# A two-layer gated convolution and MLP on one core: compact table, DMA-turned k, and a 64-row inverse

## The chip, the cores and the metric

The kernel runs on one core of one Trainium2 chip. The metric is the device time of one execution in microseconds (us), as the median over several runs. The core has a matrix engine (PE; its weight loads are listed apart as PEld), a vector engine (DVE), a scalar engine (ACT), GpSimd (POOL) and a sync engine (SP), which here issues nearly all DMAs in one queue. Each engine takes its instructions in the order in which they were written; engines wait for one another through semaphores.

## The reference, cut to what matters

Sequence length is 2048, width 512, MLP width 1376; all arrays are bf16.

```python
def A(q, k, v, shift_k, ssm_k, ssm_D):             # gated long convolution
    kv = causal_conv4(k, shift_k) * v              # 4 taps along the sequence
    y  = irfft(rfft(pad(kv)) * rfft(pad(ssm_k).T)) # causal convolution of length 2048, per channel
    return q * (y + kv * ssm_D)

def B(x, w1, b1, w2, b2):                          # MLP
    return gelu(layernorm(x) @ w1 + b1) @ w2 + b2

x = A_q
for layer in range(2):
    x = x + A(layernorm(x), A_k, A_v, A_shift_k, A_ssm_k, A_ssm_D)
    x = x + B(layernorm(x), B_w1, B_b1, B_w2, B_b2)
```

The long convolution doesn't depend on x, so that both layers use the same y. It is computed once.

## The kernel before, in words

**Halves.** The sequence is split into two halves of 1024 positions. The convolution is done by Fourier transforms of both halves, written as small matrix products; the first half of y needs only the first half of k and v, the second needs both. Positions are held as 128 partitions by 8 slices of 512 channels.

**Stages of the convolution.** For each half, tags name the stages:

- `ht0`, `ht1`: the filter `ssm_k` is turned by PE transposes (`turn`, line 536) and evicted from PSUM.
- `h1`, `x1` (`stage1`, line 553): first transform stage of the filter (h) and of the data (x): 8 tiles of 16 matmuls of 128 columns each, one eviction of 128x1024 for each tile.
- `h2`, `x2` (`stage2`, line 565): second transform stage, 8 tiles of 16 matmuls with 64 moving columns. Its weights are 128 blocks of 128x128 out of the second-stage table at `R_S2` (16,384 columns, 4 MB), which is mostly zeros: it holds, for each of 8 channels of a group, the same small rotation, in the rows and columns of that channel alone. Tile t reads 2,048 columns of it.
- `swap` (line 586 on): eight 256 KB DMAs that exchange the partitions of the real and the imaginary part of the filter's transform.
- products: DVE multiplies the two transforms (line 464, 128x1024).
- `i1` (`inverse1`, line 665): 8 tiles of 16 matmuls, 128 rows by 128 columns, with the small matrix `R_U` as moving operand; `i2` (`inverse2`, line 683): 16 matmuls of 512 columns. y of the half is then in `R_YT`.

**The short convolution.** For the first half, k is loaded by four DMAs in its natural layout and turned by 32 PE transposes (`shift_turn`, line 585) with four evictions; `shift` (line 610) does the four taps as 22 matmuls for each of four channel blocks, and DVE multiplies the result by v (line 616). For the second half, k arrives already turned, by eight transposing DMAs (line 766), and `shift_pair` (line 638) works on 32-row tiles.

**The layers.** When y of a half is there, the two layers run in blocks of 1, 2 or 4 slices (`BLOCKS`): statistics on DVE (lines 797, 798) with a power on POOL (line 804), normalization on ACT or DVE (lines 822, 823), gate and sum on DVE (line 464, 128x512), a second normalization, turning by PE or DMA, then `m1` (line 886, 44 matmuls) with the activation on ACT (line 891), and `m2` (line 920, 11 matmuls of 512 columns for each slice) with the sum on DVE (line 924). Half 0 runs its blocks while the convolution of half 1 is computed between them.

**What sets the order.** Every operation is recorded with its reads and writes by a small planner, `Prog`. The order of all operations (`SEQ`), the engine of those that may go to more than one (`ENGS`: a for ACT, v for DVE, p for POOL) and the PSUM bank of each tile (`BANKS`) are literal lists in the file; `arrange` places the operations in that order on their engines, `sync` derives the semaphore waits. So a new order is a new set of the three lists.

Of the kernel before, what the change touches and what calls it, by code (L numbers as in the profile page):

```python
# [7 lines left out]
ALU = mybir.AluOpType  # L8
# [28 lines left out]
class Prog:  # L37
# [60 lines left out]
    ENGS = ("apvpvvvpavaavaaaaaavvvaaavvvpvpvaavaaaaavaavvaaaaaaaavavaaaaaavaaavaaaaaappppaaaaaaaaaaaaaaaaaaaaaaaaaaaaapvvp"  # L98
            "paappvppaappvvvpaappaappaappaappaappaappvavpaappvappaappvvppvvvpaappvvavvvvvvavpvvvvppavavpvvvvvpvaaavpvvaaapv"
            "avva")  # L100
    BANKS = ("02220326464004602026041320002442462264542202240064064646402046462667062260046446220462640604660406064226644472"
             "44450442172316353547502206314500451400554567076567013226140174645320543403764701436154766316307007062272260403"
# [243 lines left out]
def _tables():  # L346
# [5 lines left out]
    a = np.arange(8)  # L352
# [608 lines left out]
```

## Time and profile before

| what | value |
|---|---|
| median of 3 runs | 239.39 us (238.99 to 239.71) |
| profiled execution: span from first to last instruction | 238.6 us |
| PE / DVE / ACT / POOL busy share of the span | 95% / 75% / 67% / 23% |
| DMA moved | 26.75 MB, 15.07 MB read from HBM |
| the 16 loads of the second-stage table | 256 KB each, 9.0 us from issue to landing |

The page gives the span of the profiled execution, not its device time; the median of the runs is 0.8 us longer than that span. A busy share counts an engine as busy while any of its instructions is under way; matmuls are pipelined, so that an instruction's recorded duration is much longer than the distance to the next, and distances are read from the chain or from the timeline (time of a run of instructions divided by their count). The first `m1` matmul starts 60.40 us after the span's start. In the stretch before, PE is busy in part; after it, up to 236.2 us, PE works nearly without a gap.

### The profile page before, as it was taken

To read this page: it belongs to the slowest core of one execution; us is meant where nothing else is said; L and a number is where in the kernel's file an instruction comes from. 1 tells how busy PE (TensorE), PEld (TensorE's weight loads), DVE (VectorE), ACT (ScalarE), POOL (GpSimd) and SP (SyncE) were. 2 spreads that over 40 slices of the span, in tenths; PEclk is the share of its full clock that TensorE was granted. 3 is DMA by queue.
4 is the path that set the end of the run, shared out by engine and by line. 5 is a ranking of instruction groups with operands and counts; after the bars stand their busy time and mean duration, and the time that the engine had idled before them with its cause. 6 is when DMAs were issued, how large, how long until landed. Compare 5 with 4: busy or idle time off the path is not lost.

```text
span 238.6 us, 6251 instructions
## 1 busy us (share of the span) xinstructions
PE 226.9 (95%) x2615; PEld 152.3 (64%) x2637; DVE 178.1 (75%) x358; ACT 159.6 (67%) x255; POOL 55.3 (23%) x120
## 2 busy tenths in 40 slices
PE   6998698899999999999999999999999999999995
PEld 3897588885968588667769675644445444444454
DVE  0579869999999999999999999593579469404013
ACT  2586879999996899999768786359036606831630
POOL 2421030104623506446004522303020210200000
PEclk9999979999999999999999999999999999999999
DMA  6999767989946660053100304200300050132202
GB/s 173 350 393 388 272 181 186 257 267 194 163 87 197 153 140 3 1 69 103 54 0 15 80 0 83 49 3 12 78 0 3 18 157 0 25 66 91 84 0 91
DMA packets 41112, 26.75 MB, mean 112 GB/s; under 512 B 23702, under 2 KB 33788, under 8 KB 41084
## 3 DMA queue, kind: packets, MB, share of 16 engines
q1 hardware_dynamic: 40786, 26.20, 40.5%
q8 instruction: 21, 0.34, 0.6%
q10 hardware_dynamic: 298, 0.16, 0.3%
q14 instruction: 7, 0.06, 0.1%
HBM read 15.07 MB, written 2.10 MB: 72 GB/s over the span
## 4 chain that ended last, share of the span: by engine, by line
PE 83%; DVE 6%; DMA 4%; ACT 3%; issue 2%; POOL 1%; SPq 1%; POOLq 0%
PE ps L886 32%; PE ps L920 31%; PE ps L665 6%; PE ps L553 5%; PE ps L565 3%; ACT ar L469 3%; DMA ar<-in_A_ssm_k_dram 2%; DVE ar L464 2%; DMA ar<-ar 2%; DVE ar L616 1%; PE ps L683 1%; PE ps L909 1%; PE ps L638 1%; PE ps L610 1%; DVE ar L470 1%
## 5 line engine op out<-in xcount | busy, mean ns | idle before, releaser
L891 ACT ACTIVATE ar<-ps,sm 128x256 bf16<-128x256 f32 (+4 forms) x143 | 65.4, 525 | 41.0 <-PE ps L886 39.5
L469 ACT ACTIVATE ar<-ps 128x1024 bf16<-128x1024 f32 (+3 forms) x77 | 71.3, 1005 | 16.4 <-PE ps L553 6.4
L886 PE MATMUL ps<-ar 128*128 128x256 bf16 (+4 forms) x568 | 81.5, 297 | 0.3
L920 PE MATMUL ps<-ar 128*128 128x512 bf16 (+1 forms) x324 | 77.2, 379 | 1.1 <-issue 0.3
L886 PEld LDWEIGHTS ps<-ar 128*128 128x128 bf16 (+1 forms) x572 | 52.8, 100 | 28.1 <-ACT ar L891 0.4
L464 DVE TENSOR_TENSOR ar<-ar 128x512 bf16<-128x512 bf16 (+3 forms) x105 | 62.7, 637 | 0.9 <-ACT ar L469 0.4
L920 PEld LDWEIGHTS ps<-ar 128*128 128x128 bf16 (+1 forms) x341 | 32.4, 98 | 33.4 <-ACT ar L891 0.2
L924 DVE TENSOR_TENSOR ar<-ar,ps 128x512 bf16<-128x512 bf16 x31 | 20.7, 678 | 33.2 <-PE ps L920 33.0
L797 DVE BATCH_NORM_STATS2 sm<-ar 128x6 f32<-128x512 bf16 x64 | 42.9, 683 | 0.5
L822 ACT ACTIVATE ar<-ar,sm 128x512 bf16<-128x512 bf16 x34 | 26.4, 811 | 9.5 <-DVE sm L809 8.3
L804 POOL TENSOR_TENSOR sm<-sm 128x2 f32<-128x2 f32 (+2 forms) x26 | 23.6, 909 | 23.8 <-DVE sm L802 22.0
L802 POOL TENSOR_SCALAR sm<-sm 128x2 f32<-128x2 f32 (+2 forms) x21 | 6.4, 304 | 97.3 <-DVE sm L798 97.1
L553 PE MATMUL ps<-ar 128*64 128x128 bf16 x512 | 18.6, 227 | 3.1 <-issue 1.4
L565 PEld LDWEIGHTS ps<-ar 128*128 128x128 bf16 x512 | 18.4, 102 | 3.4 <-ACT ar L469 1.0
L565 PE MATMUL ps<-ar 128*128 128x64 bf16 x512 | 19.6, 199 | 0.5 <-ACT ar L469 0.4
L553 PEld LDWEIGHTS ps<-ar 128*64 128x64 bf16 x512 | 15.7, 114 | 6.1 <-issue 2.6
L812 POOL TENSOR_SCALAR sm<-sm 128x1 f32<-128x1 f32 x43 | 16.1, 390 | 2.0
L470 DVE CAST ar<-ps 128x1024 bf16<-128x1024 f32 x11 | 13.3, 1222 | 4.3 <-PE ps L565 2.8
L665 PE MATMUL ps<-ar 128*128 128x128 bf16 x256 | 15.0, 219 | 0.5 <-DVE ar L464 0.4
L665 PEld LDWEIGHTS ps<-ar 128*128 128x128 bf16 x256 | 14.7, 113 | 1.2 <-DVE ar L464 0.6
L823 DVE TENSOR_SCALAR ar<-ar,sm 128x512 bf16<-128x512 bf16 x30 | 11.8, 410 | 3.4 <-POOL sm L812 3.1
L470 DVE COPY ar<-ps 128x1024 bf16<-128x1024 bf16 (+1 forms) x9 | 5.5, 632 | 8.0 <-PE ps L516 5.3
(41 smaller groups left out, 94.3 us busy)
## 6 DMA issues: line engine op xcount, KB each, us to landing
ar<-tab_s SPq DMA_DIRECT2D x16, 256.0 KB, 9.0
ar<-ar SPq DMA_DIRECT2D x16, 256.0 KB, 3.7
ar<-in_A_ssm_k_dram SPq DMA_DIRECT2D x8, 256.0 KB, 6.8
ar<-in_A_q_dram SPq DMA_DIRECT2D x8, 256.0 KB, 4.7
ar<-in_A_v_dram SPq DMA_DIRECT2D x8, 256.0 KB, 6.1
out_dram<-ar SPq DMA_DIRECT2D x7, 256.0 KB, 2.5
ar<-in_B_w_dram SPq DMA_DIRECT2D x4, 344.0 KB, 4.8
ar<-in_B_w_dram SPq DMA_DIRECT2D x5, 256.0 KB, 4.0
```

The source lines that it names most:

```text
L464: return P.op(eng, lambda e: e.tensor_tensor(o, a, b, op), dur, reads=[a, b] + list(more), writes=[o])
L469: return e.activation(dst, src(), AF.Copy)
L470: return e.tensor_copy(dst, src())
L553: r = e.matmul(Q(tl, 64 * ri, 64, i * 128, [1, 128]), w, m, start=True, stop=True)
L565: r = e.matmul(Q(tl, 0, 128, i // 8 * 512 + i % 8 * 4, [32, 16], [1, 4]), w, m, start=True, stop=True)
L665: r = e.matmul(Q(tl, 0, 128, i * 128, [1, 128]), w, m, start=n == 0, stop=n == 1)
L797: P.op(DVE, lambda e, sj=sj, x=x: e.bn_stats(sj, x), 600.0, reads=[x], writes=[sj])
L804: P.op(POOL, lambda e: e.tensor_tensor(r, v, hf, ALU.pow), 420.0 + 149.0 * n, reads=[v, hf], writes=[r])
L822: return e.activation(o, x, AF.Identity, bias=u, scale=r)
L886: r = e.matmul(Q(tl, 0, rows, 0, [1, w]), a, m, start=dk == 0, stop=dk == 3)
L891: P.op(ACT, lambda e, dst=dst, tl=tl, rows=rows, bias=bias, w=w: e.activation(dst, Q(tl, 0, rows, 0, [1, w]), AF.Gelu_apprx_tanh, bias=bia ...
L920: r = e.matmul(Q(tl, 0, 128, 0, [1, 512]), ins[fc][0], ins[fc][1], start=fc == 0, stop=fc == 10)
```

## The change

Four things are done together.

1. **The second-stage table is loaded compactly.** Instead of 16,384 columns, 2,048 columns are loaded (two DMAs of 256 KB, into `R_C`, which is the place of the first MLP weight `R_W1`), and 16 operations, tag `spread`, write the full table: for each half h of the table and each channel d of a group a copy of 128x1024 elements with a mask as factor, which keeps the rows of channel d and writes zeros elsewhere. Each runs on ACT, DVE or POOL; the lists give 4 to ACT, 5 to DVE and 7 to POOL. The masks are one more small POOL copy.
2. **k of the first half is turned by DMA**, as k of the second half is: eight transposing DMAs on SP's queue. The four plain loads of k, the 32 PE transposes and the four evictions go.
3. **`inverse1` of the second half works on 64-row tiles.** The rows of the transform are reordered so that the even channels of a group lie in partitions 0 to 63 and the odd ones in 64 to 127. Since `R_U` connects a channel only with itself, each 128x128x128 matmul becomes two with 64 rows, 128 weight columns and 64 moving columns, each writing its own PSUM bank. The first half keeps the old form.
4. **`SEQ`, `ENGS` and `BANKS` are new.** For instance, the first layer block `z0` alone is turned before the first `m1`, where before `z0` and `z1` both were; three of the eight `h2_1` tiles stand ahead of the first `m1`, where there were four; all evictions of the second half's `inverse1` are on ACT in both.

```diff
-    S2 = np.zeros((2, 8, 8, 128, 2, 8, 8))
-    for d in range(8):
-        S2[0, :, d, :, 0, :, d] = c
...
+    S2 = np.zeros((2, 8, 8, 128, 8, 2))
+    S2[0, :, :, :, :, 0] = c[:, None]
...
+    S2 = S2.reshape(128, 2048)
...
-    U = U.transpose(1, 2, 0, 3, 4, 5, 6).reshape(128, 256)
+    U = U[:, :, [0, 2, 4, 6, 1, 3, 5, 7]].transpose(2, 1, 0, 3, 4, 5, 6).reshape(128, 256)
...
+    sg[:, 8:] = np.arange(128)[:, None] % 8 == np.array([0, 2, 4, 6, 1, 3, 5, 7])
...
+    R_C = R_W1
...
+    for i in range(2):
+        tload(t_s2, 2048, i * 1024, R_C + i * 1024, 1024)
     load_h(0, R_1)
-    load_t(A_k, 0, R_8, 2)
+    P.tag = "kt0"
+    for a in range(8):
+        src, dst = dr(A_k, 512 * a, [8 * 512, 128], [1, 512]), A(0, 128, R_KT + 144 * a + 16, [1152, 4], [1, 128])
+        P.op(SP, lambda e, src=src, dst=dst: e.dma_start_transpose(dst, src), 1300.0, writes=[dst], dma=True, nbytes=1 << 17)
+    P.tag = ""
     load_t(A_v, 0, R_8 + 4096, 2)
-    for i in range(16):
-        tload(t_s2, 128 * 128, i * 1024, R_S2 + i * 1024, 1024)
+    P.tag = "spread"
...
+    for h in range(2):
+        for d in range(8):
+            o, c, m = A(0, 128, R_S2 + 8192 * h + 16 * d, [128, 64], [1, 16]), A(0, 128, R_C + 1024 * h, [16, 64], [1, 16]), M(0, 128, M_MK + d, [1, 1])
...
+                if e is nc.scalar:
+                    return e.activation(o, c, AF.Copy, scale=m)
+                return e.tensor_scalar(o, c, m, None, ALU.mult)
...
-    def shift_turn(c, K, kt):
...
-    for c in range(4):
-        P.tag = "fir%d" % c
-        shift_turn(c, R_8, R_KT + 1152 * c)
...
-    def inverse1(p, q, Z):
+    def inverse1(p, q, Z, split):
...
+                    if split:
+                        for g in range(2):
+                            ins.append((512 * g + 4 * i, n, A(64 * g, 64, o, [4, 128]), A(64 * g, 64, R_U + n * 128 + g, [8, 16], [2, 4])))
...
+            if split:
+                evac(BOTH, A(0, 128, Z + 64 * j, [1, 2], [512, 16], [2, 32]),
+                     lambda tl=tl: Q(tl, 0, 128, 0, [512, 2], [32, 16], [1, 32]), E1, tl)
+                continue
...
-    inverse1(R_1, R_2, R_3)
+    inverse1(R_1, R_2, R_3, False)
...
-    inverse1(HH, HI, R_Z1)
+    inverse1(HH, HI, R_Z1, True)
```

In the new order SP's queue begins so: four loads of the filter and one of q, the first part of the compact table, four transposes of k, a quarter of v, a transpose, the second part of the table, a transpose, a quarter of v, two transposes, a quarter of v, a small one, the last quarter of v. PE's queue begins so: warm-up, `ht0` and all of `h1_0`; then three of the four `shift` groups; then `h2_0`, `x1_0`, the fourth `shift` and `ht1` in alternation. DVE's begins with `ht0` and `h1_0` evictions between which five `spread` copies stand, and then comes to the `shift` products.

More of the change, by code (lines that the diff above doesn't have):

```diff
@@ L44 @@
     SEQ = (
[53 rows of a table removed]
[L98 to L102, printed above, removed]
-             "71655156407602371631706316706615043246755274432051240747516203416017010")
[55 rows of a table added]
+    ENGS = (
+            "pavvpvvppapavpppavpapvvvpaavvavaaaaaaaaaappppavvaaaaavvvvaavaaaaavaaaavaaaaavvvaaaaaaappppaaaaaaaaaaaaaa"
+            "aaaaaaaaaaavaaappvppvavvvppaappvvppaappaappaapvaappaapvaappaappavppaappaappaappvapvavppvvavpvvavvppavavp"
+            "vaavapvavvvvvvvvavvaavavvvava")
+    BANKS = (
+            "06242662440602464662026404260200245600420642204624246662204620674606220460262064222240064444666624064245"
+            "32660342504102635573724413765445521005021017064007146434254706737161257134605603001701354551741265173126"
+            "2331530057627653105537441410514013301471467740360622476437753460132260323510620")
     def __init__(self, nc):
@@ L356, in _tables @@
     c, s = np.cos(th), np.sin(th)
-    S2 = np.zeros((2, 8, 8, 128, 2, 8, 8))
-    for d in range(8):
-        S2[0, :, d, :, 0, :, d] = c
-        S2[1, :, d, :, 0, :, d] = s
-        S2[0, :, d, :, 1, :, d] = -s
-        S2[1, :, d, :, 1, :, d] = c
-    S2 = S2.transpose(0, 1, 2, 3, 5, 6, 4).reshape(128, 128 * 128)
+    S2 = np.zeros((2, 8, 8, 128, 8, 2))
+    S2[0, :, :, :, :, 0] = c[:, None]
+    S2[1, :, :, :, :, 0] = s[:, None]
+    S2[0, :, :, :, :, 1] = -s[:, None]
+    S2[1, :, :, :, :, 1] = c[:, None]
+    S2 = S2.reshape(128, 2048)
     ph = TWO_PI * k2[:, None] * a[None, :] / 8
@@ L439, in bass_interleave_layers__ssm_conv_h3__mixer_channel_mlp__prompt_kernel @@
     R_HRAW1, R_HP1, R_G1, R_HS1, R_K1, R_Z1 = R_W2, R_KT, R_8, R_8, R_1, R_1
+    R_C = R_W1
     R_D, R_W, R_TR = R_W2 + 4096, R_W2 + 4608, R_W2 + 5120
-    M_B1, M_ST, M_MV, M_RS, M_HF, M_NM, M_SG = 0, 16, 208, 240, 256, 260, 276
-    assert M_SG + 1 <= NS
+    M_B1, M_ST, M_MV, M_RS, M_HF, M_NM, M_SG, M_MK = 0, 16, 208, 240, 256, 260, 276, 284
+    assert M_MK + 8 <= NS
     F, S2, U, T2, sg = _tables()
@@ L491, in load_t, with f @@
             dma(A(0, 128, o + 512 * a, [1, 512 * w]), dr(x, 512 * (1024 * half + a), [8 * 512, 128], [1, 512 * w]), w << 17, paced=True)
+    for i in range(2):
+        tload(t_s2, 2048, i * 1024, R_C + i * 1024, 1024)
     load_h(0, R_1)
-    load_t(A_k, 0, R_8, 2)
-    load_t(A_v, 0, R_8 + 4096, 2)
-    for i in range(16):
-        tload(t_s2, 128 * 128, i * 1024, R_S2 + i * 1024, 1024)
+    P.tag = "kt0"
[3 more added lines that the diff above has]
+    P.tag = ""
+    load_t(A_v, 0, R_8 + 4096, 2)
+    P.tag = "spread"
+    mk, src = M(0, 128, M_MK, [1, 8]), A(0, 128, R_SG + 8, [1, 8])
+    P.op((DVE, POOL), lambda e, mk=mk, src=src: e.tensor_copy(mk, src), {DVE: 65.0, POOL: 190.0}, reads=[src], writes=[mk])
+    for h in range(2):
+        for d in range(8):
+            o, c, m = A(0, 128, R_S2 + 8192 * h + 16 * d, [128, 64], [1, 16]), A(0, 128, R_C + 1024 * h, [16, 64], [1, 16]), M(0, 128, M_MK + d, [1, 1])
+            def f(e, o=o, c=c, m=m):
+                if e is nc.scalar:
+                    return e.activation(o, c, AF.Copy, scale=m)
+                return e.tensor_scalar(o, c, m, None, ALU.mult)
+            P.op((ACT, DVE, POOL), f, {ACT: 912.0, DVE: 340.0, POOL: 1200.0}, reads=[c, m], writes=[o])
+    P.tag = ""
     tload(t_sm, row, 464, R_U, 256)
@@ L576, in swap @@
                     dma(dst, src, 1 << 18, reads=[src])
-    def shift_turn(c, K, kt):
-        tl = Tile(1)
-        src = [A(0, 128, K + 512 * a + 128 * c, [1, 128]) for a in range(8)]
-        def f(e, src=src, tl=tl):
-            for a in range(8):
-                r = e.transpose(QB(tl, 0, 128, a * 128, [1, 128]), src[a], IDN)
-            return r
-        P.op(PE, f, 8 * 56.0, reads=src + [IDN], tile=tl)
-        evac(BOTH, A(0, 128, kt + 16, [144, 8], [1, 128]), lambda tl=tl: QB(tl, 0, 128, 0, [128, 8], [1, 128]), EB, tl)
     def shift(half, c, K, V):
@@ L660, in inverse1 @@
                 for n, r in enumerate((p, q)):
-                    ins.append((i, n, A(0, 128, r + (dg // 4) * 512 + dg % 4, [4, 128]), A(0, 128, R_U + n * 128, [1, 128])))
+                    o = r + (dg // 4) * 512 + dg % 4
+                    if split:
+                        for g in range(2):
+                            ins.append((512 * g + 4 * i, n, A(64 * g, 64, o, [4, 128]), A(64 * g, 64, R_U + n * 128 + g, [8, 16], [2, 4])))
+                    else:
+                        ins.append((i * 128, n, A(0, 128, o, [4, 128]), A(0, 128, R_U + n * 128, [1, 128])))
             def f(e, ins=ins, tl=tl):
                 for i, n, w, m in ins:
-                    r = e.matmul(Q(tl, 0, 128, i * 128, [1, 128]), w, m, start=n == 0, stop=n == 1)
+                    r = e.matmul(Q(tl, 0, 128, i, *([32, 16], [1, 4]) if split else ([1, 128],)), w, m, start=n == 0, stop=n == 1)
                 return r
-            P.op(PE, f, 16 * 56.0, reads=[x for y in ins for x in y[2:]], tile=tl)
+            P.op(PE, f, 32 * 18.0 if split else 16 * 56.0, reads=[x for y in ins for x in y[2:]], tile=tl)
+            if split:
+                evac(BOTH, A(0, 128, Z + 64 * j, [1, 2], [512, 16], [2, 32]),
+                     lambda tl=tl: Q(tl, 0, 128, 0, [512, 2], [32, 16], [1, 32]), E1, tl)
+                continue
             evac(BOTH, A(0, 128, Z + 64 * j, [512, 16], [8, 8], [1, 8]),
```

108 rows, old and new, of the table SEQ are left out of this document.

## The prediction

> **What bounds the kernel now.** I read the page's header, shares and slices first, then the busy time by stage, then the chain of waits in order of time.
>
> ```profile
> span 238.6 us, 6251 instructions
> ...
> PEclk9999979999999999999999999999999999999999
> DMA  6999767989946660053100304200300050132202
> ```
> ```profile
> 8.50:17.70 9.20, 9.20 (x217) 8.63 (x218) 6.19 (x9) 6.83 (x7) 2.63 (x8) 1.00 1.05 389
> 17.74:60.40 42.66, 36.88 (x804) 31.91 (x801) 39.12 (x65) 37.10 (x42) 8.33 (x24) 0.96 0.87 247
> 60.40:124.90 64.50, 63.76 (x904) 48.13 (x914) 63.90 (x112) 56.23 (x112) 23.82 (x40) 1.00 0.40 88
> 124.90:236.20 111.30, 110.71 (x665) 60.03 (x673) 67.53 (x170) 57.08 (x93) 17.98 (x39) 1.00 0.17 43
> ```
> ```profile
> 8.58 3.80 PE ps L553 x92
> ...
> 13.03 1.79 PE ps L585 x32
> ...
> 15.83 1.89 PE ps L610 x44
> 17.72 0.02 issue
> 17.74 2.36 DVE ar L616 x2
> ...
> 30.59 3.38 PE ps L565 x64
> ...
> 56.54 0.20 POOL sm L802
> ...
> 57.47 0.28 POOL sm L812
> ...
> 59.86 0.49 ACT ar L469
> 60.35 0.05 issue
> 60.40 3.97 PE ps L886 x68
> 64.37 0.47 PE ps L565 x16
> ...
> 72.12 1.05 PE ps L638 x87
> ...
> 124.95 0.90 PE ps L665 x16
> ...
> 126.49 6.26 PE ps L665 x112
> ```
>
> The columns of the stage table after the length are PE, PEld, DVE, ACT and POOL busy, granted clock, DMA share, GB/s. Two parts show. From 60.40 us, the first `m1` matmul, to 236.2 PE is busy 174.5 of 175.8 us: there the time is PE's work, and a microsecond of it saved is a microsecond. DVE is as full as PE up to 124.9 (63.90 of 64.50) and has slack only behind. Before 60.40 no engine is full all the time: DMA is (share 1.05) while the table comes in, then DVE (39.12 of 42.66) and ACT (37.10) share the load, PE waits between. So the kernel is: the moment T1 of the first `m1`, plus the PE work left then, plus a tail of 2.4 us. I price the change as a shift of T1 and a change of the work behind it.
>
> **Behind T1: the 64-row inverse.** Before, 128 matmuls of `i1_1` take 0.90 + 6.26 = 7.16 us, 55.9 ns each. After, 256 with 64 columns. Bounds: the 32-row tiles of L638, with 93 moving columns in the mean (eleven matmuls share 32 pieces of 32), come every 1.05/87 = 12.1 ns, which gives 3.1 us; L565, 64 columns on all rows and so one at a time, comes every 0.47/16 = 29.4 ns, which gives 7.5 us. Nearest is L610, also two 64-row tiles side by side: 1.89/44 = 43 ns at 186 columns in the mean (32 pieces of 64); by columns alone that is 14.8 ns at 64. The weights are read with a step of four elements, and such a load is longer:
>
> ```profile
> L665 PEld LDWEIGHTS ps<-ar x256: 111/113/133, 43.9 to 132.5; 128*128 128x128 bf16 x128
> ```
> ```profile
> L565 PEld LDWEIGHTS ps<-ar x512: 95/98/132, 23.3 to 110.4; 128*128 128x128 bf16 x171
> ```
> ```profile
> L469 ACT ACTIVATE ar<-ps 128x1024 bf16<-128x1024 f32 x67 | 64.2, 1041 | 10.3 <-PE ps L553 6.4 <-PE ps L665 2.3 <-PE ps L565 1.4
> ```
>
> 113 against 98 ns. I put 17 ns a matmul: 4.4 us, a saving of 2.8. The eight evictions are of the same size and on ACT as before; m1 and m2 matmuls fill PE between the tiles. If that filler were gone, eight evictions in a row (L469, 1.04 us each) would bind, and nearly all of the saving would go. The new order moves work behind T1: one more `h2_1` tile (0.47 us) and the four transposes of `z1` (0.2 us, by L585's 1.79/32). Net: 2.1 us less.
>
> Here the Trainium skill speaks against the change: "TensorE: Matmul & The Clock Gate", "Wait — 56ns, not 53.3ns?", says that matmuls don't start closer than about 25 ns however few their columns. By that rule the estimate would be 256 x 25 ns = 6.4 us, a saving of 0.8 in place of 2.8. The trace disagrees for tiles side by side (12.1 ns).
>
> **Ahead of T1.** The rows:
>
> ```profile
> 0.73 1.33 SPq L449 DMA_DIRECT2D ar<-in_A_ssm_k_dram  x3
> ```
> ```profile
> L766 SPq DMA_TRANSPOSE ar<-in_A_k_dram x8: 1195/1268/2090, 52.9 to 64.6; - x8
> ...
> DMA to landing us min/median/max: 3.0/4.5/5.6
> ```
> ```profile
> L449 SPq DMA_DIRECT2D ar<-in_A_v_dram x4: 328/580/1741, 49.8 to 71.5; - x4
> ...
> DMA to landing us min/median/max: 3.5/4.0/4.8
> ```
> ```profile
> L470 DVE CAST ar<-ps 128x1024 bf16<-128x1024 f32 x9 | 10.9, 1223 | 3.1 <-PE ps L565 2.8 <-PE ps L553 0.3
> L464 DVE TENSOR_TENSOR ar<-ar 128x1024 bf16<-128x1024 bf16 x16 | 9.9, 682 | 0.0
> L797 DVE BATCH_NORM_STATS2 sm<-ar 128x6 f32<-128x512 bf16 x9 | 6.1, 683 | 0.0
> L616 DVE TENSOR_TENSOR ar<-ps,ar 128x1024 bf16<-128x1024 f32 x4 | 4.7, 1214 | 1.5 <-PE ps L610 1.5
> ...
> L798 DVE BATCH_NORM_AGGREGATE sm<-sm 128x2 f32<-128x6 f32 x10 | 1.7, 177 | 0.1
> L823 DVE TENSOR_SCALAR ar<-ar,sm 128x512 bf16<-128x512 bf16 x4 | 1.6, 406 | 0.0
> ```
> ```profile
> L523 POOL TENSOR_TENSOR ar<-ar 128x256 bf16<-128x256 bf16 x4 | 2.4, 612 | 4.2 <-DVE ar L470 4.0
> ```
>
> *SP's queue.* A plain issue takes 1.33/3 = 0.44 us, a transpose 1.27. Six plain ones end at 0.73 + 2.7 = 3.4. Until the eighth transpose stand seven others (with gaps 9.1) and three plain ones (1.3): it is issued at 13.8 and lands 4.5 later, at 18.3 (16.8 to 19.4). The last quarter of v is issued at 16.0 and lands at 20.0 (19.5 to 20.8). Before, k and v were among the first loads, and the first tap matmuls stand at 15.83. So removing the table's 14 loads frees the DMAs but not the start of the taps: what is late next is k and v themselves, behind transposes that are long to issue.
>
> *Taps.* One group is 22 matmuls, 0.95 us. DVE's first product needs the second group and all of v: 18.3 + 1.9 = 20.2, and 20.0. But `h1_0` is done at about 13 (92 of its 128 matmuls end at 12.4 above), and in the new order PE has nothing else: it stands five microseconds. In the slice at 30 us the clock row falls to 7, and the 64 matmuls there come at 53 ns in place of 29.4. With that clock a group takes 1.7 us, and the product starts at 21.7. I take 21.0, against 17.74 before: 3.3 us later. The same page of the skill ("Part 1: The HAM clock gate") has the clock halved after an idle window of about 3.4 us; the trace agrees in kind, the 7 standing behind a shorter gap.
>
> *From there to T1* DVE carries the chain in its written order. Up to the statistics of `z0` it has 4 products (1.18 each), 16 transform products (0.62), 8 evictions from f32 (1.21), 4 turned-filter evictions (0.69, as L797's size), 7 statistics (0.68), 7 operations on 512 columns (0.41) and 10 small ones (0.17): 4.7 + 9.9 + 9.7 + 2.8 + 4.8 + 2.9 + 1.7 = 36.5 us, and I add 1.0 of waiting for the second exchange of the filter's halves. In the old order 17.74 to 56.5, 38.8 us, lay between the same points. Then POOL's three operations for `z0` (56.54 to 57.75, 1.2), normalization (0.4), transposes (0.2), eviction (0.49), gaps 0.1: 2.4 in place of 3.9, since `z1` no longer stands in front. T1 = 21.0 + 37.5 + 2.4 = 60.9, 0.5 later than 60.40.
>
> *The copies.* Five on DVE: 1024 elements, two bounds, 0.41 (L823, half the size) and 0.68 (L464, two sources); I take 0.6, 3.0 in all, before 20 us, where DVE is not full (6.19 of 9.20 above). But one stands ahead of two `h1_0` evictions and needs the second part of the table, issued at 11, landed at 15.5: copy, eviction, copy, eviction end at 19.1. These evictions free the banks of the taps; with 21.0 they are covered, from 2 us more on they aren't. Four on ACT: 1.04 as L469, or up to 1.2 with a factor per row: 4.5 us, in ACT's wait for the taps, ending at 19. Seven on POOL: L523 gives 2.4 ns an element with two sources, so 2.4 us at most; with one source half of that, 1.2 us, is my value; 1.0 to 2.4. The last POOL copy that tiles 0 to 3 of `h2_0` need ends at 18 to 20, behind the taps' own POOL work; the last of all ends at 25 to 30, and tiles 4 to 7 start at about 32. The first part of `R_W1` can be loaded only behind the last copy; SP's queue stops there, with the exchange of the filter's halves behind it, which needs evictions of about 30 us anyway. Removed beside: 32 transposes and four evictions, which lay at 12 to 17 us, where nobody waited for PE.
>
> *Sum.* 238.6 + 0.5 - 2.1 = 237.0 of span. The profiled execution's own time isn't in the page; its span stands 0.8 below the median of the runs, 239.39, and I add that: **237.8 us**.
>
> **Rivals.**
>
> *The front gains too.* If the transposes land at their minimum, the clock stays and v comes at 19.5, the product starts at 19.5; without DVE's waiting T1 is 58.4, and the time 235.3. For it: with the table gone DMA has room. Against it: the issue times on SP, which no room shortens.
>
> *The taps come late (slower).* Transposes between other loads have taken up to 2.09 us to issue. At 1.5 us each the eighth is issued at 15.4; with the longest landing, 5.6, and the slow clock the second group ends at 24.4; with the product at 24.5 the time is 237.8 + 3.5 = 241.3. No other work is in front of the chain to take this up. It decides from a first product at 23.3 us on: there the time passes 240.1. For it: DVE and ACT are full from there to T1 and can't catch up.
>
> *The 64-row tiles don't run side by side.* If weight loads with a step keep the two halves apart, 256 matmuls at 29.4 ns take 7.5 us, the saving of 2.8 turns into a loss of 0.4, and the time is 241.0: slower by half a percent. Against it: L610 and L638, both with weights in a row. The skill's 25 ns above would mean 239.8.
>
> **How the numbers follow.** Chances: forecast 0.46 (own range 235.8 to 239.8, by the landings, by 12 to 22 ns a matmul); gain in front too 0.2; late taps 0.2; no overlap 0.14. Range 234.3 to 241.5: it reaches past the centres of the rivals and leaves 2 in 10 out. A measurement can tell about 0.3%, 0.7 us, from no change: 238.7 to 240.1 counts as the same. Faster: three quarters of the first and all of the second case, 0.56. Slower: most of the last two, 0.29. Same: 0.15.
>
> **What would show it.** Right: the last transpose landing at 17 to 19.5, the first L626 product at 20 to 22 us, a stretch of about 5 us without matmuls ahead of the taps, T1 at 59.5 to 62, `i1_1` at 15 to 20 ns a matmul, PE full from T1 on. Wrong: a product before 19 or behind 23.3; copies on POOL behind which `h2_0` or SP's queue waits; `i1_1` near 28 ns; or PE gaps behind T1, for DVE has no slack there either and the new order may feed its blocks worse.

## The result, and the profile after

The changed kernel takes 255.71 us (255.25 to 257.99, four runs) beside 239.55 us for the kernel before in the same session: a ratio of 1.0708, 95% interval 1.0656 to 1.076. It is 16 us slower; 237.8 was forecast, and the range ended at 241.5. The profiled execution has a span of 253.6 us against 238.6, that is 15.0 us to be found.

From the changed kernel's page: the span, the row of granted clock in 40 slices, and the shares of the chain by engine, where PE stood at 83% before.

```profile
span 253.6 us, 6459 instructions
...
PEclk9976995979999999999999999999999999999999
...
PE 51%; POOL 15%; DVE 13%; ACT 11%; DMA 4%; issue 3%; SPq 2%; POOLq 0%; DVEq 0%
```

The timeline of its PE gives the marks that the prediction used (start, duration, line, and in brackets the idle time ahead with what ended it): taps, the first tile of `h2_0` that needs the second half of the table, `i1_0`, the first `m1`, the first `i1_1`.

```profile
17.98 5.30 PE L620 MATMUL ps<-ar 64*128 64x256 bf16 x66 [4.44 <-DMA ar<-in_A_k_dram]
...
35.80 0.63 PE L587 MATMUL ps<-ar 128*128 128x64 bf16 x16 [3.16 <-POOL ar L517]
...
53.42 8.96 PE L680 MATMUL ps<-ar 128*128 128x128 bf16 x128 [2.13 <-DVE ar L469]
...
70.83 1.07 PE L902 MATMUL ps<-ar 128*128 128x128 bf16 x16 [1.13 <-ACT ar L474]
...
139.04 2.99 PE L680 MATMUL ps<-ar 64*128 64x64 bf16 x160
```

T1 is 70.83 in place of 60.40 (+10.4). From T1 to the first `i1_1` matmul it takes 68.2 us in place of 64.4 (124.78 - 60.40; +3.8). From there to the end 114.6 in place of 113.8 (+0.7). So nearly all of the loss lies ahead of `i1_1`. There the busy time of VectorE tells most. The stage tables below are of the kernel before and then of the changed one: from 20 us to the first `i1_1`, then from the first tap product to the end of `z0`'s statistics, and for the changed kernel from `i1_1` to the end (after the length: PE, PEld, DVE, ACT, POOL busy, clock, DMA share, GB/s).

```profile
20.00:124.78 104.78, 98.71 (x1654) 78.37 (x1662) 100.64 (x175) 93.04 (x153) 32.16 (x63) 0.98 0.58 147
17.74:56.46 38.72, 33.79 (x733) 29.48 (x731) 35.18 (x58) 33.20 (x37) 5.17 (x15) 0.96 0.85 259
```
```profile
20.00:139.04 119.04, 105.95 (x1729) 82.66 (x1727) 102.30 (x172) 92.08 (x150) 45.00 (x65) 0.94 0.44 118
21.61:66.93 45.32, 36.70 (x729) 32.14 (x726) 34.83 (x57) 32.01 (x35) 20.44 (x24) 0.87 0.56 163
139.04:253.60 114.56, 111.34 (x812) 57.97 (x811) 67.72 (x173) 63.04 (x99) 15.79 (x33) 1.00 0.17 42
```

DVE has 101 to 102 us of work in that stretch in both kernels. Before, it stood 4.1 us (104.78 - 100.64); now it stands 16.7. That is 12.6 of the 15 us. What it waited for longest in the changed kernel from 20 us to the first `i1_1` (waiting line, releaser, us, times, longest):

```profile
DVE sm L825 <- POOL sm L820: 5.2, 1, 5.2
DVE ar L469 <- DMA ar<-ar: 4.6, 2, 2.5
DVE ar L626 <- PE ps L620: 3.1, 1, 3.1
DVE ar L469 <- ACT ar L474: 1.5, 2, 0.9
```

The first is a small operation of `q1`, whose power stands on POOL behind the last copy of the table. The second are the exchanges of the filter's halves, in both halves of the sequence. The copies themselves, on POOL and on DVE:

```profile
L517 POOL TENSOR_SCALAR ar<-ar,sm x7: 2842/2842/2854, 11.3 to 32.8; 128x1024 bf16<-128x1024 bf16 x7
L517 DVE TENSOR_SCALAR ar<-ar,sm x5: 477/648/1033, 8.4 to 16.8; 128x1024 bf16<-128x1024 bf16 x5
```

And SP's queue: it stands at the load into `R_W1` until the last copy is done (32.81 + 2.85 = 35.66), and the exchanges come behind it.

```profile
35.68 0.82 SPq L454 DMA_DIRECT2D ar<-in_B_w_dram  x2
36.54 0.72 SPq L454 DMA_DIRECT2D ar<-ar  x1
```

The chain of waits that ended last runs over POOL from the first copy on, and reaches DVE only at 36.41 us:

```profile
11.33 2.86 POOL ar L517
...
32.81 2.85 POOL ar L517
...
35.80 0.59 POOL sm L820
36.39 0.02 issue
36.41 0.16 DVE sm L825
```

The first reading was plain: POOL's copies cost 2.84 us, not 1.2, and this is the loss. The experiments show that it isn't so plain.

### The profile page after: what moved, and what is told of

It reads as the page before. It is cut to its first block, busy times and chain, and to the rows that moved or that the text cites. A ratio compares the mean times of both kernels' runs of the same rounds, so it can differ in the third digit from the quotient of the medians.

```text
span 253.6 us, 6459 instructions
## 1 busy us (share of the span) xinstructions
PE 229.9 (91%) x2733; PEld 149.6 (59%) x2733; DVE 180.1 (71%) x360; ACT 166.5 (66%) x259; POOL 73.0 (29%) x121
## 4 chain that ended last, share of the span: by engine, by line
PE 51%; POOL 15%; DVE 13%; ACT 11%; DMA 4%; issue 3%; SPq 2%; POOLq 0%; DVEq 0%
PE ps L902 21%; PE ps L936 21%; POOL ar L517 8%; ACT ar L474 8%; DVE ar L469 6%; DMA ar<-ar 4%; PE ps L680 3%; POOL sm L828 2%; POOL sm L820 2%; ACT ar L838 2%; PE ps L587 2%; DVE sm L813 2%; SPq L454 2%; PE ps L702 1%; DVE ar L475 1%
## 5 line engine op out<-in xcount | busy, mean ns | idle before, releaser
L902 PE MATMUL ps<-ar 128*128 128x256 bf16 (+5 forms) x572 | 82.1, 297 | 2.7 <-DMA ar<-ar 1.2
L936 PE MATMUL ps<-ar 128*128 128x512 bf16 (+1 forms) x341 | 79.8, 379 | 1.7 <-ACT ar L907 1.2
L838 ACT ACTIVATE ar<-ar,sm 128x512 bf16<-128x512 bf16 x38 | 30.0, 819 | 9.4 <-DVE sm L825 5.1
L820 POOL TENSOR_TENSOR sm<-sm 128x2 f32<-128x2 f32 (+2 forms) x26 | 22.0, 847 | 27.9 <-DVE sm L818 25.9
L587 PEld LDWEIGHTS ps<-ar 128*128 128x128 bf16 x512 | 19.1, 104 | 6.8 <-issue 3.3
L517 POOL TENSOR_SCALAR ar<-ar,sm 128x1024 bf16<-128x1024 bf16 x7 | 19.9, 2845 | 0.7
L680 PE MATMUL ps<-ar 64*128 64x64 bf16 (+1 forms) x384 | 13.9, 211 | 2.6 <-DVE ar L469 2.1
L475 DVE CAST ar<-ps 128x1024 bf16<-128x1024 f32 (+1 forms) x12 | 14.0, 1172 | 3.0 <-PE ps L702 1.1
L680 PEld LDWEIGHTS ps<-ar 64*128 64x128 bf16 (+1 forms) x384 | 13.4, 117 | 3.5 <-DVE ar L469 2.3
L828 POOL TENSOR_SCALAR sm<-sm 128x1 f32<-128x1 f32 x33 | 14.3, 449 | 1.6
```

Source lines behind the costliest of these rows:

```text
L517: return e.tensor_scalar(o, c, m, None, ALU.mult)
L587: r = e.matmul(Q(tl, 0, 128, i // 8 * 512 + i % 8 * 4, [32, 16], [1, 4]), w, m, start=True, stop=True)
L680: r = e.matmul(Q(tl, 0, 128, i, *([32, 16], [1, 4]) if split else ([1, 128],)), w, m, start=n == 0, stop=n == 1)
L820: P.op(POOL, lambda e: e.tensor_tensor(r, v, hf, ALU.pow), 420.0 + 149.0 * n, reads=[v, hf], writes=[r])
L838: return e.activation(o, x, AF.Identity, bias=u, scale=r)
L902: r = e.matmul(Q(tl, 0, rows, 0, [1, w]), a, m, start=dk == 0, stop=dk == 3)
```

## The experiments

All ratios are to the kernel before on the same chip, with 95% intervals. "Idle" is DVE's idle time from 20 us to the first `i1_1` matmul. T1 and idle come from one trace of each kernel. The kernel before, the inverse alone and its form with other evictions (below) have the same work in the same order ahead of T1, and T1 is 60.4, 59.2 and 58.2 there, so differences of 2 us in T1 tell little.

| kernel | ratio | T1 | T1 to `i1_1` | idle |
|---|---|---|---|---|
| before | 1 | 60.4 | 64.4 | 4.1 |
| changed | 1.0708 (1.0656 to 1.076) | 70.8 | 68.2 | 16.7 |
| copies on DVE, new order | 1.0716 (1.0664 to 1.0767) | 68.4 | 71.7 | 19.0 |
| cheap copies on POOL, new order | 1.0781 (1.07 to 1.0863) | 68.6 | 71.5 | 18.9 |
| copies on DVE, k plain, new order | 1.0551 (1.0505 to 1.0598) | 65.8 | 71.5 | 17.2 |
| inverse alone, old order | 1.0061 (1.0033 to 1.009) | 59.2 | 64.5 | 4.2 |
| and compact table, copies on DVE, old order | 1.0101 (1.0049 to 1.0152) | 62.5 | 64.5 | 4.2 |
| and k by DMA: all parts, old order | 1.0206 (1.0152 to 1.0259) | 63.3 | 64.5 | 4.5 |
| the same, seven copies on POOL | 1.0673 (1.0621 to 1.0725) | 73.9 | 64.5 | 15.0 |
| new order up to T1, old behind | 1.0559 (1.0512 to 1.0606) | 71.9 | 64.2 | 13.5 |
| old order up to T1, new behind | 1.0791 (1.0738 to 1.0845) | 64.6 | 76.0 | 17.5 |

### The copies taken off GpSimd

```diff
+        for i, e in ((29, DVE), (30, DVE), (26, DVE), (37, DVE), (32, DVE), (35, DVE), (36, DVE)):
+            self.ops[i].eng = e
```

In `SEQ` operations 29, 30, 26 also go ahead of 34, and 37, 32, 35, 36 behind 75.

> The changed kernel with its seven GpSimd copies of the table made by VectorE instead, early in VectorE's order; all else as changed. Theory A (the price of the GpSimd copies, 2.84 us each, and what queues behind them): first m1 matmul at 61 to 64.5 us instead of 70.8; the whole 246 to 249 us if the gaps behind that moment have a cause of their own, 240 to 243 if they came from the late table too. Rival B (the new order, with k turned by DMA, is late by itself): first m1 at 67 us or later, the whole over 251.

Measured: 256.55 us, ratio 1.0716, first `m1` at 68.4. That is what rival B expected, and the whole is as slow as with GpSimd's copies. DVE's waits in this kernel, over the same stretch:

```profile
DVE ar L471 <- DMA ar<-ar: 7.3, 3, 3.2
DVE ar L471 <- ACT ar L476: 4.2, 1, 4.2
DVE ar L628 <- PE ps L622: 2.6, 1, 2.6
```

The wait for POOL is gone, and the waits for the exchanges and for ScalarE have grown by what it took (4.6 to 7.3, 1.5 to 4.2). DVE comes earlier to the exchange and finds it still under way: for the longest of these waits ahead of T1 it is there at 44.0 us and goes on at 47.2, in the changed kernel at 48.2 and 50.3. Theory A, that the copies' price is the loss, falls for the new order.

### No copies at all: the whole table loaded

```diff
-    for i in range(2):
-        tload(t_s2, 2048, i * 1024, R_C + i * 1024, 1024)
...
+    for i in range(16):
+        tload(t_s2, 16384, i * 1024, R_S2 + i * 1024, 1024)
```

> The changed kernel without the compact table and its copies: the whole 4 MB table comes by 16 loads again, issued on the DMA queue behind the last v load; k by DMA transposes, inverse and order as changed. Theory A (the copies' price): first m1 at 61 to 65 us, the whole 240 to 248. Rival B (order and transposes): first m1 at 67 or later, the whole over 251. If the 16 loads come later than the chain needs them, TensorE waits for a DMA ahead of the stage 2 tiles, and the row says so.

Measured: ratio 1.1293 (1.1241 to 1.1344). This run tells nothing about the copies: the 16 loads, issued behind the transposes, hold up the filter's second half, and PE stands for that. Its longest wait up to 60 us:

```profile
PE ps L547 <- DMA ar<-in_A_ssm_k_dram: 12.9, 2, 12.5
```

### What a copy on GpSimd costs, by its form

```diff
+                if e is nc.gpsimd:
+                    k = form[0] = form[0] + 1
+                    if k == 1:
+                        r = e.tensor_scalar(spare, A(0, 128, R_C + 1024 * h, [1, 1024]), m, None, ALU.mult)
...
```

> A price list, not a candidate: in the changed kernel each of the seven GpSimd copies of the table is followed by a second GpSimd instruction on the same 128x1024 bf16 elements into a spare place, each in another form: destination in one run instead of steps; the factor as a constant; a plain copy; half as many elements; a product of two tensors; a plain copy into steps; a memset. If the price of 2.84 us lies in the destination's steps, the dense forms take 1.0 to 1.4 us; if it lies in the factor read from a register column, the constant and the plain copy take 1.0 to 1.4; if it is GpSimd's rate for 16-bit elements in any two-operand form, all but the memset stay at 2.3 to 3.0 and the half one takes 1.4 to 1.6.

The timeline of POOL in that run (start, duration):

```profile
11.37 2.86 POOL L518 TENSOR_SCALAR ar<-ar,sm 128x1024 bf16<-128x1024 bf16 x1
14.21 2.85 POOL L522 TENSOR_SCALAR ar<-ar,sm 128x1024 bf16<-128x1024 bf16 x1
...
20.01 2.77 POOL L524 TENSOR_SCALAR ar<-ar 128x1024 bf16<-128x1024 bf16 x1
...
27.91 1.04 POOL L526 COPY ar<-ar 128x1024 bf16<-128x1024 bf16 x1
...
33.19 1.57 POOL L528 TENSOR_SCALAR ar<-ar,sm 128x512 bf16<-128x512 bf16 x1
...
37.66 1.90 POOL L530 TENSOR_TENSOR ar<-ar 128x1024 bf16<-128x1024 bf16 x1
...
42.44 1.04 POOL L532 COPY ar<-ar 128x1024 bf16<-128x1024 bf16 x1
```

L518 is the copy as the change has it, L522 the same with a dense destination, L524 with a constant factor, L526 a plain copy, L532 a plain copy into steps. Neither the steps nor the factor's column sets the price; the operation with a scalar does. A product of two tensors is cheaper than a product with a number. None of the three expected causes is right as worded.

### The cheap form in the changed kernel

```diff
+                if e is nc.gpsimd:
+                    return e.tensor_copy(o, c)
                 return e.tensor_scalar(o, c, m, None, ALU.mult)
```

> The changed kernel, its order and engines untouched, but each of the seven GpSimd copies is a plain copy without the factor (the mask is left out of them, so that part of the computation is left out); the price list has that form at 1.04 us, next to the 1.2 us that my prediction took. If the price was the only step of the prediction that failed, first m1 comes at 60 to 63 us and the whole at 238 to 243. If the step on the late taps failed too (TensorE standing for k costs the front 4 us that my sum took as covered) and the new order loses 3 us behind the first m1, first m1 comes at 65 to 68 and the whole at 248 to 252.

Measured: 256.82 us, ratio 1.0781. First `m1` at 68.6, the whole above both theories. With copies of 1.04 us, under the price that I had taken, the changed kernel is no faster. So the price alone does not explain the miss. `i1_0` in the kernel before, and in this run:

```profile
43.91 7.63 PE L665 MATMUL ps<-ar 128*128 128x128 bf16 x128 [0.41 <-DVE ar L464]
```
```profile
50.46 9.71 PE L682 MATMUL ps<-ar 128*128 128x128 bf16 x128 [5.12 <-DVE ar L469]
```

PE stands 5.1 us for DVE, which stands for the exchange, and the 128 matmuls then take 9.7 us in place of 7.63.

### k not turned

```diff
-        src, dst = dr(A_k, 512 * a, [8 * 512, 128], [1, 512]), A(0, 128, R_KT + 144 * a + 16, [1152, 4], [1, 128])
-        P.op(SP, lambda e, src=src, dst=dst: e.dma_start_transpose(dst, src), 1300.0,
+        src, dst = dr(A_k, 512 * a, [8 * 512, 128], [128, 4], [1, 128]), A(0, 128, R_KT + 144 * a + 16, [1152, 4], [1, 128])
+        P.op(SP, lambda e, src=src, dst=dst: e.dma_start(dst, src), 1300.0,
...
```

> The changed kernel with its GpSimd copies, but the eight DMA transposes of the first half of k are plain loads to the same places (k stays unturned, so that part of the computation is left out). Theory B1 (TensorE, and ScalarE behind it, stand 4 to 5 us for the eighth transpose, issued at 1.27 us each, and nothing later gives that back): first m1 at 64 to 67 us instead of 70.8, the whole 248 to 252. Theory A1 (the GpSimd copies hold the middle tiles of h2_0 whatever k does): first m1 stays at 69 to 71, the whole 253 to 257.

> Both causes taken away: the GpSimd copies made by VectorE, and k of the first half loaded plainly (unturned, that part of the computation left out). If two covers hide each other (either cause alone is enough to make the first swap late), first m1 comes at 60 to 64 us and the whole at 240 to 247, though each cause taken away alone gave little. If the written order is late by itself, first m1 stays at 66 or later and the whole above 250.

Measured: with GpSimd's copies 1.0746 (1.07 to 1.0791), no faster than the changed kernel, so theory B1 falls. With the copies on DVE 251.79 us, 1.0551: the whole is over 250, as the second case has it, T1 at 65.8 is just below its bound, and idle is still 17.2. Both suspects gone, 13 us are left. The inverse accounts for little of them (below), so most belong to the written order.

### The inverse alone, and the order in which its evictions write

The kernel before with the 64-row form in the second half and the table's columns to suit; in the other run the eviction is changed as well:

```diff
-    inverse1(HH, HI, R_Z1)
+    inverse1(HH, HI, R_Z1, True)
...
-                evac(BOTH, A(0, 128, Z + 64 * j, [1, 2], [512, 16], [2, 32]),
-                     lambda tl=tl: Q(tl, 0, 128, 0, [512, 2], [32, 16], [1, 32]), E1, tl)
+                evac(BOTH, A(0, 128, Z + 64 * j, [512, 16], [2, 32], [1, 2]),
+                     lambda tl=tl: Q(tl, 0, 128, 0, [32, 16], [1, 32], [512, 2]), E1, tl)
```

> The kernel before with one part of the change alone: the second half's inverse on 64-row tiles, with the table's columns in the order it wants. My prediction's price (4.4 us less 2.8 of matmul time saved, less 0.7 behind it): 236.5 to 238.5 us. Rival C (the evictions with a destination step of two elements bind, about 1.2 us each for eight): 238.5 to 240.5, no gain, and in the chain of waits a row of eight ScalarE evictions over 9 us.

> As the run with the inverse alone, but each of the eight evictions writes its destination in rising order (the same places, source read with the step instead). If the step of the destination is what makes them slow (rival C), an eviction takes 0.95 to 1.05 us instead of 1.2 to 1.33 and the whole falls 1 to 2 us below that run; if the eight evictions take the same time in either order, the two runs agree within 0.5 us.

Measured: 240.83 us, ratio 1.0061, and 237.92 us, ratio 0.9954 (0.9927 to 0.998). ScalarE's evictions of `i1_1` in the kernel before, with the inverse alone, and with the rising order:

```profile
127.43 6.52 ACT L469 ACTIVATE ar<-ps 128x1024 bf16<-128x1024 f32 x7 [0.52 <-PE ps L665]
```
```profile
124.47 9.83 ACT L469 ACTIVATE ar<-ps 128x1024 bf16<-128x1024 f32 x8 [0.96 <-PE ps L670]
```
```profile
124.82 6.52 ACT L469 ACTIVATE ar<-ps 128x1024 bf16<-128x1024 f32 x7 [0.39 <-PE ps L670]
```

0.93 us each before, 1.23 with the change, 0.93 again when the same places are written in rising order (the source in PSUM is then read with the step). Rival C holds, with the whole 0.3 us above its range. The version with the rising order takes 0.5% less than the kernel before (0.2 to 0.7%). What binds in it is seen on PE: three tiles of `i1_1` start 0.92 us apart, 0.72 of it matmuls and 0.20 a wait for ScalarE's eviction.

```profile
126.81 0.72 PE L670 MATMUL ps<-ar 64*128 64x64 bf16 x32 [0.20 <-ACT ar L469]
127.73 0.72 PE L670 MATMUL ps<-ar 64*128 64x64 bf16 x32 [0.20 <-ACT ar L469]
```

### Both halves' inverses on 64-row tiles

```diff
-    inverse1(R_1, R_2, R_3, False)
+    inverse1(R_1, R_2, R_3, True)
```

> A candidate: the kernel before with the inverse of both halves on 64-row tiles and evictions that write in rising order. The first half's inverse takes 7.4 to 7.6 us on TensorE in the kernel before and lies ahead of the first m1 with nothing beside it. If its matmuls bind, it falls by 3 us and the whole comes to 235 to 236.5; if its eight evictions on ScalarE and VectorE bind (about 1 us each on two engines), it falls by 1 us or less, 237 to 238.

Measured: 241.24 us, ratio 1.0117 (1.0063 to 1.0171): slower than either case expected. `i1_0` lasts 9.4 us on PE, where the 128-row form took 7.38 in the run with the rising order. PE waits for the evictions, the longest time for one on DVE:

```profile
49.45 1.90 PE L670 MATMUL ps<-ar 64*128 64x64 bf16 x64 [2.32 <-DVE ar L470]
```

### All parts in the old order

`SEQ`, `ENGS` and `BANKS` are those of the kernel before, renumbered; the transposes and loads of the front in the new order on SP; copies set in on DVE and ACT.

```diff
-        48, 0, 6, 51, 213, 2, 8, 40, 1, 7, 41, 3, 194, 9, 4, 16, 22, 50, 10, 13, 17, 58, 42, 43, 19, 59, 44, 55, 12,
+        6, 8, 7, 9, 4, 16, 10, 13, 17, 19, 12, 5, 15, 20, 14, 11, 21, 18, 40, 41, 213, 1, 51, 0, 22, 42, 43, 2, 46,
...
```

> All three parts of the change (compact table spread by VectorE and ScalarE, twelve copies and four; k of the first half by DMA transposes; the second half's inverse on 64-row tiles) in the order of the kernel before on every engine, with the copies set in where their engines stood idle. The run with the copies on VectorE in the new order took 256.6 us. Theory D (the new order is what is late): first m1 at 62 to 65 us, the whole 242 to 247. Rival B (the transposes hold TensorE, whatever the order): first m1 at 66 or later, the whole over 250.

> The same without the DMA transposes: k of the first half is loaded and turned on TensorE as in the kernel before; the compact table by copies on VectorE and ScalarE, and the second half's inverse on 64-row tiles, in the order of the kernel before. The run with the inverse alone took 240.8 us. If the copies hide in the idle time of VectorE (about 4 us before its first tap product) and ScalarE, 240 to 242; if their 12 x 0.52 us delay the tap products, 243 to 246. What the run in the old order with transposes takes above this one is the price of the transposes.

> All three parts in the order of the kernel before, with seven copies on GpSimd as the change has it, its tap tables put ahead of them. Their 7 x 2.84 us end at 31 to 33 us if they run without a gap from 11. Theory D (order): the whole within 2 us of the run in the old order with the copies on VectorE, since the second half of the table is wanted about there. If the GpSimd price decides by itself, the middle tiles of h2_0 wait again and the whole comes 4 us or more above that run.

Measured: 1.0337 (1.029 to 1.0385) for all parts, 247.31 us with T1 at 66.5, so the whole is nearer to theory D and T1 to rival B; 1.0101 without the transposes; 1.0517 (1.0453 to 1.0582) with seven copies on POOL, 5 us above the first, so their price does decide here. The order matters. But the first and the third run had a fault of mine: the first block of q was issued behind the transposes, and DVE stood for it.

```profile
DVE sm L815 <- DMA ar<-in_A_q_dram: 8.0, 1, 8.0
```

So the load was put back to its place:

```diff
-        6, 8, 7, 9, 4, 16, 10, 13, 17, 19, 12, 5, 15, 20, 14, 11, 21, 18, 40, 41, 213, 1, 51, 0, 22, 42, 43, 2, 46,
+        6, 8, 7, 194, 9, 4, 16, 10, 13, 17, 19, 12, 5, 15, 20, 14, 11, 21, 18, 40, 41, 213, 1, 51, 0, 22, 42, 43, 2,
...
```

> The run in the old order with all three parts and the copies on VectorE (247.3 us), with one load moved: the first block of q, which VectorE's first statistics wait for, is issued fourth on the DMA queue as in the changed kernel; in that run it stood behind the transposes, and VectorE waited 8.0 us for it until 22.40. Theory V (VectorE is the bound from 20 us to the first matmul of the second half's inverse, and only its idle time counts): about 4 to 6 us of that wait come back, the whole at 241 to 244, and the transposes are then worth at most 2 us. Rival B (TensorE standing for k is what costs): the whole stays at 246 or more.

> The same with seven copies on GpSimd as the change has them (252.4 us with the late load of q). Theory V: VectorE still waits 5 us or more for the power on GpSimd that stands behind the copies, so the whole is 4 to 6 us above the run with the copies on VectorE: 245 to 250. If the price of the copies is hidden in this order, the two agree within 1.5 us.

> A candidate: the run in the old order with the early q, with the inverse's evictions writing in rising order. From the pair of runs on the eviction: 1.5 to 2.9 us below that run, 239 to 242; below 238.5 it would beat the kernel before.

Measured: 244.55 us (1.0206), 255.59 us (1.0673), 242.59 us (1.0132; 1.0066 to 1.0198). The first gained 2.8, less than theory V asked; the second lies 11 us above the first, twice what I expected, and 3 above the same kernel with the late q; the third doesn't beat the kernel before. With POOL's copies, DVE waits for the power behind them, in one piece:

```profile
DVE sm L825 <- POOL sm L820: 11.1, 1, 11.1
```

### One order ahead of T1, the other behind

All parts, copies on DVE; the first 312 operations of the new `SEQ` and the rest in the old one, and the reverse, whose first lines are shown.

```diff
-        48, 0, 6, 51, 213, 2, 8, 40, 1, 7, 41, 3, 194, 9, 4, 16, 22, 50, 10, 13, 17, 58, 42, 43, 19, 59, 44, 55, 12,
+        6, 8, 7, 194, 9, 4, 16, 10, 13, 17, 19, 12, 5, 15, 20, 14, 11, 21, 18, 40, 41, 213, 1, 51, 0, 22, 42, 43, 2,
...
```

> All three parts, copies on VectorE. Up to the first m1 matmul every engine follows the new order, behind it the order of the kernel before. Whole new order 256.6 us, whole old order 244.6. Behind the first m1 the new order took 71.7 us to the first matmul of the second half's inverse, the old 64.5. If the loss lies in both stretches, as VectorE's waits say (5 us for swaps ahead of it; 2.5 for a swap and 4.2 behind ScalarE after it), this comes to 248 to 251. If the back is long only because the front left more for it, it stays at 254 to 257.

> The other half: the order of the kernel before up to the first m1, the new order behind it. If the new order's back loses by itself, 249 to 252; if the new back is as good as the old once the front is in time, 243 to 246.

Measured: 252.07 us (1.0559) and 257.23 us (1.0791). The first lies between its two cases, the second above both of its own. Both stretches lose by themselves, but the losses don't add up to that of the whole new order (1.0716), and the seam belongs to neither order, so a part of each may be the seam's. In all eleven profiles with the old order behind T1 (the kernel before among them) it takes 64.2 to 64.5 us to the first `i1_1`, whatever T1 was; with the new order 68.2 to 76.0. With the old front and the new back, DVE's waits between T1 and `i1_1`:

```profile
DVE ar L471 <- ACT ar L476: 3.9, 1, 3.9
DVE ar L471 <- DMA ar<-ar: 3.8, 1, 3.8
DVE ar L772 <- PE ps L589: 3.5, 2, 3.3
```

In the kernel before, the only wait of DVE in that stretch is 0.4 us, for PE.

## Why the prediction was wrong

**Where it failed: DVE's chain to T1, "and I add 1.0 of waiting".** The prediction took T1 as the first tap product, plus DVE's work of 36.5, plus 1.0, plus 2.4. From that product to the end of `z0`'s statistics the table above has 45.32 us, of which DVE is busy 34.83. The work was 1.7 us less than my sum. The waiting was 10.5: 5.2 for the power on POOL behind the copies, 2.1 for an exchange, 2.9 for PE. The kernel before waits 3.5 us between the same points (38.72, busy 35.18), so that 1.0 was low even for it. From there to T1 it took 3.90, as before (3.94), and not 2.4: `z0` alone is turned, but its eviction stands on ACT behind a normalization of `q3`, until 70.20. So T1 = 21.61 + 45.32 + 3.90 = 70.83, against 21.0 + 37.5 + 2.4 = 60.9. I priced DVE's operations and not its waits, and up to 36.4 us the chain was not even DVE's but that of POOL's copies.

Between the predicted span of 237.0 and the measured 253.6 lie 16.6 us: 9.9 ahead of T1, 3.1 from T1 to `i1_1` (64.38 + 0.7 expected, 68.21 measured) and 3.5 behind (113.82 - 2.8 expected, 114.56 measured).

**The POOL copies, 1.2 us, bounds 1.0 to 2.4.** Measured 2.84, above the upper bound. I had halved a row of a product of two tensors because the copy has one source; the price list shows that a product with a scalar is dearer than one of two tensors. The rest of the step fell with it: not "25 to 30" but 35.7 for the last copy, with tiles of `h2_0`, SP's exchanges and the power of `q1` queued behind. The prediction named the first two as signs of being wrong and did not see the third. What this is worth depends on the rest: 1.0206 against 1.0673, 11 us, in the old order (5 with the late q), nothing in the new one.

**"+0.7 moved behind T1."** Between T1 and `i1_1` the new order costs 3.8 us in the changed kernel, and 7 to 12 with the copies on DVE. The prediction's last sentence had "the new order may feed its blocks worse" as a sign and gave it no time and no rival. PE is busy 64.95 of these 68.21 us, so that it did stand there for 3.3.

**The inverse, 2.8 saved.** 160 matmuls in 2.99 us are 18.7 ns each, against 17 predicted, so the rival in which the tiles don't run side by side is out; so is the 25 ns between matmuls of the Trainium skill ("TensorE: Matmul & The Clock Gate", "Wait — 56ns, not 53.3ns?") for tiles of this kind. But the evictions, "of the same size and on ACT as before", are not the same: 1.23 in place of 0.93. Alone, the part costs 0.6% where a gain was forecast; with evictions in rising order it gains 0.5%, 1.1 us, less than the 2.8 forecast, since the evictions at 0.93 us then set the pace of the tiles. The prediction had `m1` and `m2` matmuls fill PE between the tiles, and said that without them the evictions would bind; so it came.

**What was right.** The taps start at 17.98 when the last transpose of k lands (18.3 predicted); PE stands 4.4 us ahead of them (five); the clock row is down behind it; the first product is at 21.61 (21.0). ACT's copies (1.14) and the median of DVE's (0.65) lie within their bounds.

**Rivals.** None of them came true. The slower one, late taps, decided at a first product of 23.3, and it was 21.61. The case that happened, a chain that starts in time and then waits, was not among them.

**The sum, as measured.** In the old order: the inverse +0.6%, the compact table with copies on DVE and ACT +0.4% more (within the intervals), the transposes of k +1.05% (the intervals touch). On top of these 2.1%, 5 us, the new order alone adds 5.1%, and GpSimd's copies alone add 4.7%; both together add 5.0%. Each is enough, and they don't add up: both make the same engine wait in the same stretch, and a wait that starts later finds the exchange landed or nearly so. That the waits replace each other is seen in DVE's rows above. (GpSimd's copies also stand at other places of the order than DVE's, and the intervals are about 0.5% to each side.) What in the new order puts DVE at an exchange too early stays open. With the copies on DVE in both, the exchanges are issued no later in the new order than in the old (the first from 32.3 us against 33.2, the second four from 39.0 against 38.5). But seven weight loads stand on SP from 36.4 to 48.3 us, where the old order has the first of them at 44.0, and the exchange on the chain to T1 took 6.8 us to land against 3.7. No run moved those loads.

## What to carry to other kernels

Where one in-order engine is full through a stage, sum its waits, not only its work: ask at each of its instructions what comes from another queue, and whether it is there. A suspect whose removal changes nothing isn't cleared: take the suspects away together and one by one, and put them singly into the old kernel, since each of two can be enough. Price an instruction by a row of the same operation and operand kinds, and an eviction by the order in which it writes.

## What the runs showed of the hardware

- GpSimd on 1024 bf16 elements a partition: plain copy 1.04 us, product of two tensors 1.90, product with a scalar 2.77 to 2.89 (1.57 for 512), with the steps of the destination making no difference. The Trainium skill ("GPSIMD Engine Reference", "4.1 Engine selection") has one-input work at roughly line rate and two-input work slower. The copy, 1.04 beside 1.90, agrees in kind; the product with a scalar, one input and 2.84, does not.
- ScalarE wrote the same 128x1024 eviction in 0.93 us in rising order and in 1.23 when consecutive elements go two places apart; the order of the source changed with it, and the two were not separated.
- After a stand of 5.1 us the same 128 matmuls took 9.7 us, after 0.4 us 7.63.
- Sixteen 256 KB loads ahead of it in the queue made a load of the filter 12.5 us late for PE.
